# Changed loads, casts and sketch order in a polysketch attention and tanh-shrink FFN kernel

## The chip, the cores and the metric

The kernel runs on one core of a Trainium2 chip. The metric is the device time of one execution in microseconds (us); lower is better. Before the change it is 114.17 us, the median of three runs (113.98 to 114.34).

## What is computed

There are 4 batches, 4 heads, 1088 tokens and a head dimension of 32. The attention is linear: each q and k row is sketched by two 8 x 32 matrices, and the feature vector is the outer product of the two sketches (64 features).

```python
def phi(x):
    a = np.einsum('rd,bhsd->bhsr', S1, x)
    b = np.einsum('rd,bhsd->bhsr', S2, x)
    return np.einsum('bhsi,bhsj->bhsij', a, b).reshape(*x.shape[:-1], r * r)
q_p, k_p = phi(q), phi(k)
kv  = np.einsum('bhsf,bhsd->bhfd', k_p, v)
z   = np.sum(k_p, axis=2)
num = np.einsum('bhsf,bhfd->bhsd', q_p, kv)
den = np.einsum('bhsf,bhf->bhs', q_p, z)[..., None] + 1e-06
attn = num / den
```

The result, as x of shape 4352 x 128, goes through a layer without a gate, with w_in 128 x 2048 and w_out 2048 x 128:

```python
h = x @ w_in
out = (h - np.tanh(h)) @ w_out
```

## The kernel before, in words

**Order of the work.** The kernel does not issue instructions directly. Each step is added to a program (`P.add`) with the engines that may run it, an estimated duration, what it reads and writes, and a key (its priority). A list scheduler, `schedule`, then walks through an estimated time and gives every engine a fixed, in-order queue; `sync` adds the semaphores. An instruction that waits thus holds up everything behind it on its engine. Where TensorE would be idle in the plan, `fill` puts 128x256 matmuls on zeros (line 435) into its queue. The durations and the due times (`T_FIRST`, `PERIOD`, the keys) are constants at the top of the file.

**Loads.** All loads are added by `load` (line 466), in one order: k, q's first 8 of 34 chunks, v of batch 0; then the first quarter of W_in, the rest of q, three quarters of W_in, four quarters of W_out; then k, q and v of batches 1 to 3. They are issued by SyncE (the two small sketch matrices by ScalarE). `CAP` (1.4e6 bytes) bounds what is under way: a load waits for the landing of the one that would bring the sum over it. W_in comes in rows of 2 KB, W_out in pieces of 512 bytes. Both are f32 and are cast to bf16 in `weights` by ScalarE or GpSimd.

**Attention of a batch.** Here is the chain, with the names that the prediction uses.
- *kT, qT*: VectorE transposes k and q in blocks of 32 x 32 (lines 583, 592).
- *k sketch, kab*: TensorE multiplies by the sketch matrices (lines 599 and 610), VectorE transposes the result into `abk` (line 616).
- *gram, gm, scmm, sc*: small products that give what the denominator needs (lines 638, 642, 625, 648). From batch 1 on, scmm stands at the head of the kv product.
- *w*: three outer products on VectorE (line 659). *kv*: TensorE multiplies them by v (line 671). *kvd, kvt, kvb*: copy, transpose on TensorE, copy (lines 375, 703, 375).
- *q sketch, abc*: TensorE (line 724), then a VectorE transpose (line 729). *m, den, rd, ap*: the denominator and the divided sketch, on VectorE (lines 741 to 749).
- *qp, qpT*: outer products and their transposes on VectorE, 512 or 768 columns at a time (lines 767, 772). *num*: TensorE (line 783). *x*: two copies out of PSUM into the bf16 x, by VectorE or ScalarE (line 375).

Batch 0 is cut so that the first two of its nine blocks of 128 tokens give an early x: first k, w, kv and q's first piece, then the other seven blocks. The pieces in which num and x are done are in `PIECES`.

**FFN.** The 4352 rows of x are cut into ten groups of 256, 384, 448, six times 512, and 192. For each group, 16 *h* matmuls (line 877) each feed a tanh on ScalarE (line 881), and 16 + 2 *o* matmuls (lines 892, 896) sum up the output; the h @ w_out part is folded into one product W_c = w_in @ w_out, split into two bf16 halves, `wch` and `wcl` (lines 855 to 861; *wit* and *wiT* are the transposes of W_in that it needs). VectorE transposes the output (*ot*, line 901), and SyncE stores it. In the last three groups one tanh takes two banks (128 x 1024). The h matmuls use three PSUM banks, so TensorE can be three of them ahead of ScalarE.

Of the kernel before, what the change touches and what calls it, by code (L numbers as in the profile page):

```python
# [6 lines left out]
DM = 128  # L7
DFF = 2048
NJB = DFF // 128
NC = 34  # L10
# [12 lines left out]
CAP = 1.4e6  # L23
PAIRS = 7
URGENT = (-60500.0, 450.0)
PIECES = {0: [(0, 2), (2, 5), (5, 9)], 1: [(0, 5), (5, 9)], 2: [(0, 9)], 3: [(0, 9)]}
# [65 lines left out]
class _Prog:  # L92
# [58 lines left out]
    def schedule(self, filler=None):  # L151
# [31 lines left out]
        while n < len(self.ops):  # L183
# [33 lines left out]
            if e == "tensor":  # L217
                if o.name == "o0.0":
                    fills = False
# [7 lines left out]
            if o.dma:  # L227
                free[e] = t + occ
                wire = max(t + 1450.0, wire) + o.dma
                o.t1 = wire + (300.0 if o.key < -79000 else 2000.0)  # L230
            else:
                o.t1 = t + occ
                free[e] = o.t1
# [17 lines left out]
    def fill(self, filler, a, b):  # L251
        t = a
        while t + FILL[0] + FILL[1] < b:
            o = _Op()
            o.engs = {"tensor": (FILL[0], 215.0)}
# [3 lines left out]
            o.eng, o.t0, o.t1, o.lat = "tensor", t, t + FILL[0], 215.0  # L259
# [86 lines left out]
def bass_polysketch_attn__then__act_tanh_shrink_kernel(  # L346
# [43 lines left out]
    kL = [sb("kL", [128, NC * 32]) for _ in range(B)]  # L390
    vL = [sb("vL", [128, H, NB * 32]) for _ in range(B)]
    qL = [sb("qL", [128, NC * 32]) for _ in range(B)]
# [16 lines left out]
    NTH = 20  # L409
# [16 lines left out]
    wo_f = sb("wo_f", [128, NJB, DM])  # L426
    wi = [sbv("wi", [128, 512], BF16) for _ in range(4)]
    wo = [sbv("wo", [128, 4, DM], BF16) for _ in range(4)]
# [32 lines left out]
    for b in range(B):  # L461
        P.add(_v(128), lambda e, n, b=b: e.memset(vL[b][64:128, :, 256:288], 0.0), w=[vvals[b][1]], key=-89000 + b)
# [3 lines left out]
    def load(key, o_, i_, w, nbytes, eng="sync", rate=330.0, cap=True):  # L466
        after = []
        if cap:
            left = CAP - nbytes
            for op, nb in reversed(loads):  # L470
                left -= nb
                if left < 0:
                    after = [op]
                    break
        op = P.add({eng: (450.0, 0.0)}, lambda e, n: e.dma_start(out=o_, in_=i_), w=w, key=key, dma=nbytes / rate,
# [4 lines left out]
    for x, Sx in ((0, S1), (1, S2)):  # L480
        load(-99000 + x, sin.ap[:, x, :], Sx[None, :, :].to_broadcast([16, 8, 32]), [sin], 16384, "scalar")

    kvals = [[_Val(ap=kL[b].rearrange("p (r x) -> p r x", r=2)[:, :, e * 288:(544 if e else 288)]) for e in range(2)] for b in range(B)]
    qcut = {0: [0, 8, 34]}
# [3 lines left out]
    def load_k(key, b):  # L488
        src = k[b].rearrange("h (t r c) d -> (h t) r (c d)", r=2, c=17)
        if b == 0:  # L490
            for e in range(2):
                load(key + e, kvals[b][e].ap, src[:, :, e * 288:(544 if e else 288)], [kvals[b][e]], 128 * (256 if e else 288) * 8)
        else:
            load(key, kL[b][:, :], k[b].rearrange("h (t c) d -> (h t) (c d)", c=NC), kvals[b], 128 * 1088 * 4)

    def load_v(key, b):
        vs = v[b].rearrange("h (m x) d -> m h (x d)", x=17)
        for e in range(2):
            w_ = 256 if e else 288
            load(key + e, vL[b][e * 64:(e + 1) * 64, :, 0:w_], vs[:, :, e * 288:e * 288 + w_], [vvals[b][e]], 64 * w_ * 16)  # L500

    def load_q(key, b, i):
        a, z, val = qvals[b][i]
        src = q[b].rearrange("h (t c) d -> (h t) (c d)", c=NC)
        load(key, qL[b][:, a * 32:z * 32], src[:, a * 32:z * 32], [val], 128 * (z - a) * 128)

    wif = [_Val(ap=wi_f[:, i * 512:(i + 1) * 512]) for i in range(4)]
    wof = [_Val(ap=wo_f[:, i * 4:(i + 1) * 4, :]) for i in range(4)]
    wos = moe_w_out.rearrange("(jb ji) c -> ji jb c", jb=NJB, ji=128)

    def load_wi(key, i):
        load(key, wif[i].ap, moe_w_in[:, i * 512:(i + 1) * 512], [wif[i]], 128 * 2048)

    def load_wo(key, i):
        load(key, wof[i].ap, wos[:, i * 4:(i + 1) * 4, :], [wof[i]], 128 * 2048)
# [5 lines left out]
    load_wi(next(lk), 0)  # L521
    load_q(next(lk), 0, 1)
    for i in range(1, 4):
        load_wi(next(lk), i)
    for i in range(4):
        load_wo(next(lk), i)
    for b in range(1, B):
        load_k(next(lk), b)
        load_q(next(lk), b, 0)
        load_v(next(lk), b)  # L530

# [33 lines left out]
    xvals = []  # L565
    seq = [0]
# [6 lines left out]
    kT = [_Val(kT_p) for _ in range(B)]  # L573
    abk = [_Val(abk_p) for _ in range(B)]
# [5 lines left out]
    def k_transposes(b):  # L580
        for e_ in range(2):
            nb = NB - e_
            P.add(_v(nb * 64), lambda e, n, e_=e_, nb=nb: e.transpose(  # L583
                kT[b].ap.rearrange("p (j u t r) -> p r j u t", u=2, t=32, r=2)[:, :, 0:nb, e_, :],
                kL[b].rearrange("p (r j t) -> p r j t", r=2, t=32)[:, :, e_ * 9:e_ * 9 + nb, :]),
                r=[kvals[b][e_]], w=[kT[b]], key=nk(), name=f"kT{b}.{e_}")
# [7 lines left out]
    def k_sketch(b):  # L594
        _, pk = _group(att2, 2)
        for rh in range(2):
            def sk(e, n, rh=rh):
# [393 lines left out]
```

## Time and profile before

| what | us |
|---|---|
| median of three runs | 114.17 |
| the profiled execution | 114.65 |
| its span in the trace | 112.6 |
| TensorE matmul busy | 100.3 |
| ScalarE busy | 79.9 (tanh 69.5) |
| VectorE busy | 72.1 |
| GpSimd busy | 5.6 |
| first x complete | 18.96 |
| first tanh | 20.03 |
| last x copied from | 83.68 |

The span is the time between the first and the last instruction that the trace shows; some 2 us of the execution lie outside it. Times on a line of a timeline are counted from the start of the span. A line of a timeline gives the start, the duration, the engine, the source line, the operation, output and input and their number, and in brackets how long the engine was idle before and for whom. The chain of waits is followed back from the last instruction: at each step to what released it. Busy time of TensorE overlaps in the records, so that a TensorE shown as busy may still have room.

### The profile page before, as it was taken

How to read it: one execution, taken by the hardware profiler on the slowest of the kernel's cores; microseconds unless marked ns; L12 is line 12 of the kernel's file. 1: busy time of each engine (PE TensorE's matmuls, PEld its weight loads, DVE VectorE, ACT ScalarE, POOL GpSimd, SP SyncE). 2: the span in 40 equal slices, each digit the busy share in tenths (PEclk: the TensorE clock that was granted, in tenths of full speed). 3: DMA queues.
4: the chain of work that ended last, by engine and by line, in shares of the span. 5: the costliest groups of instructions: out<-in, count | busy, mean ns of one | idle time of the engine just before them, and what ended most of it. 6: DMA issues, size and time to landing. Idle time of an engine off the chain costs nothing.

```text
span 112.6 us, 3409 instructions
## 1 busy us (share of the span) xinstructions
PE 100.3 (89%) x1467; PEld 48.7 (43%) x1477; DVE 72.1 (64%) x115; ACT 79.9 (71%) x164; POOL 5.6 (5%) x25
## 2 busy tenths in 40 slices
PE   6975996998799989979999999979999999999960
PEld 4523783455355444436443346334243334334540
DVE  4469374899999999999999992499950020020030
ACT  2101247876487798586599867798969999999950
POOL 5202016000000000000000000000000000000000
PEclk9999999999999999999999999999999999999999
DMA  1999878799987804022000230005004106005035
GB/s 21 259 245 329 255 232 234 243 241 272 226 270 218 165 5 69 0 47 46 0 6 0 44 49 6 6 11 83 0 6 68 25 0 93 0 12 77 4 55 73
DMA packets 25037, 11.24 MB, mean 100 GB/s; under 512 B 18880, under 2 KB 23616, under 8 KB 25024
## 3 DMA queue, kind: packets, MB, share of 16 engines
q1 hardware_dynamic: 24320, 10.97, 40.7%
q8 instruction: 11, 0.18, 0.7%
q10 hardware_dynamic: 704, 0.08, 0.5%
q14 instruction: 2, 0.02, 0.1%
HBM read 8.81 MB, written 2.23 MB: 98 GB/s over the span
## 4 chain that ended last, share of the span: by engine, by line
PE 36%; ACT 28%; DVE 16%; DMA 13%; issue 2%; SPq 1%; DVEq 0%
ACT th L881 25%; PE psb L892 11%; PE psb L877 10%; DMA qL<-in_q_dram 5%; DMA wo_f<-in_moe_w_out_dram 5%; PE psb L783 5%; DVE qp L767 4%; DVE qpT L772 4%; DVE abc L729 3%; DMA kL<-in_k_dram 3%; PE psb L724 3%; PE psb L671 3%; DVE ot L901 2%; PE psb L610 2%; ACT wiT L375 2%
## 5 line engine op out<-in xcount | busy, mean ns | idle before, releaser
L881 ACT ACTIVATE th<-psb 128x512 bf16<-128x512 f32 (+4 forms) x136 | 69.5, 624 | 7.4 <-PE psb L877 6.6
L877 PE MATMUL psb<-xT,wi 128*128 128x512 bf16 (+4 forms) x155 | 50.1, 349 | 1.5 <-DVE xT L375 0.5
L892 PE MATMUL psb<-th,wo 128*128 128x512 bf16 (+4 forms) x157 | 48.2, 348 | 1.4 <-DVE ot L901 0.6
L877 PEld LDWEIGHTS psb<-xT,wi 128*128 128x128 bf16 x160 | 14.9, 97 | 25.3 <-ACT th L881 14.4
L892 PEld LDWEIGHTS psb<-th,wo 128*128 128x128 bf16 x160 | 14.6, 97 | 15.7 <-ACT th L881 7.5
L901 DVE STREAM_TRANSPOSE ot<-psb 128x512 f32<-128x512 f32 (+4 forms) x10 | 6.3, 626 | 22.6 <-PE psb L892 22.6
L772 DVE STREAM_TRANSPOSE qpT<-qp 128x768 f32<-128x768 f32 (+1 forms) x14 | 12.1, 861 | 0.4
L767 DVE TENSOR_TENSOR qp<-ap,abc 128x768 f32<-128x768 f32 (+1 forms) x14 | 11.5, 818 | 0.1
L659 DVE TENSOR_TENSOR w<-abk 128x768 f32<-128x768 f32 x12 | 11.3, 981 | 0.1
L729 DVE STREAM_TRANSPOSE abc<-psb 128x1152 f32<-128x1152 f32 (+2 forms) x5 | 5.7, 1143 | 5.1 <-PE psb L724 5.0
L435 PE MATMUL psb<-zz 128*128 128x256 bf16 x33 | 7.8, 388 | 1.1 <-DVE zz L434 1.1
L783 PE MATMUL psb<-qpT,kvb 32*32 32x128 f32 (+4 forms) x448 | 8.3, 309 | 0.1
L375 ACT CAST xT<-psb 128x192 bf16<-128x192 f32 (+4 forms) x8 | 3.3, 421 | 5.4 <-PE psb L783 5.4
L583 DVE STREAM_TRANSPOSE kT<-kL 128x576 f32<-128x576 f32 (+1 forms) x8 | 5.6, 724 | 1.7 <-DMA kL<-in_k_dram 1.7
L783 PEld LDWEIGHTS psb<-qpT,kvb 32*32 32x32 f32 x448 | 5.1, 103 | 2.9 <-DVE qpT L772 2.0
L671 PE MATMUL psb<-w,vL 128*32 128x64 f32 x288 | 6.0, 243 | 0.0
L592 DVE STREAM_TRANSPOSE qT<-qL 128x1088 f32<-128x1088 f32 (+2 forms) x5 | 5.3, 1055 | 0.9 <-DMA qL<-in_q_dram 0.9
L435 PEld LDWEIGHTS psb<-zz 128*128 128x128 bf16 x33 | 4.1, 135 | 3.6 <-DVE zz L434 1.1
L671 PEld LDWEIGHTS psb<-w,vL 128*32 128x32 f32 x288 | 5.1, 125 | 0.3 <-issue 0.2
L642 ACT COPY gm<-psb 128x32 f32<-128x32 f32 x4 | 0.8, 198 | 5.6 <-PE psb L638 5.6
L724 PE MATMUL psb<-qT,wq 32*32 32x288 f32 (+2 forms) x160 | 3.6, 381 | 0.9 <-ACT xT L375 0.9
L375 DVE CAST xT<-psb 128x192 bf16<-128x192 f32 (+3 forms) x6 | 2.8, 467 | 1.1 <-PE psb L783 1.0
(55 smaller groups left out, 56.6 us busy)
## 6 DMA issues: line engine op xcount, KB each, us to landing
kL<-in_k_dram SPq DMA_DIRECT2D x3, 544.0 KB, 3.6
qL<-in_q_dram SPq DMA_DIRECT2D x3, 544.0 KB, 4.9
vL<-in_v_dram SPq DMA_DIRECT2D x4, 288.0 KB, 4.8
vL<-in_v_dram SPq DMA_DIRECT2D x4, 256.0 KB, 5.0
wi_f<-in_moe_w_in_dram SPq DMA_DIRECT2D x4, 256.0 KB, 4.7
wo_f<-in_moe_w_out_dram SPq DMA_DIRECT2D x4, 256.0 KB, 5.8
out_dram<-ot SPq DMA_DIRECT2D x16, 64.0 KB, 2.0
out_dram<-ot SPq DMA_DIRECT2D x8, 56.0 KB, 1.9
```

The costliest lines, as they stand in the source:

```text
L375: return e.copy(o, i) if name == "scalar" else e.tensor_copy(o, i)
L435: filler = (lambda e, n: e.matmul(bank(3)[:, 0:256], zz.ap[:, 0:128], zz.ap[:, 128:384], start=True, stop=True), zop)
L659: P.add(_v(768), lambda e, n: e.tensor_tensor(out=wv.ap.rearrange("p (x i j) -> p x i j", i=8, j=8), in0=abh(0)[:, :, :, None].to_broadcas ...
L671: i = e.matmul(pv[b].ap[h * 32:(h + 1) * 32, 0:64], vL[b][:, h, blk * 32:(blk + 1) * 32], wvs[b, p].ap[:, (bi * 4 + h) * 64:(bi * 4 + h + ...
L729: P.add(_vp(sn * 4), lambda e, n: e.transpose(abc.ap.rearrange("p k h f -> p h k f")[:, :, 0:s1 - s0, :], psa4[:, :, 0:sn].rearrange("p h ...
L767: P.add(_v(cn * 256), lambda e, n, qp=qp, c0=c0, cn=cn: e.tensor_tensor(out=qp.ap[:, 0:cn * 256].rearrange("p (x i j) -> p x i j", i=8, j= ...
L772: P.add(_v(cn * 256), lambda e, n, qp=qp, o0=o0, cn=cn: e.transpose(qt.ap[:, o0 * 256:(o0 + cn) * 256], qp.ap[:, 0:cn * 256]), r=[qp], w=[ ...
L783: i = e.matmul(psa4[h * 32:(h + 1) * 32, g, 0:nb * 32], kvb.ap[g * 32:(g + 1) * 32, x, h * 32:(h + 1) * 32], qq[g * 32:(g + 1) * 32, 0:nb, ...
L877: P.add(_pe(n_ / 2.4 + 2.6), lambda e, n, jb=jb, hv=hv: e.matmul(hv.ap[:, jb % m * 512:jb % m * 512 + n_], wi[jb // 4].ap[:, (jb % 4) * 12 ...
L881: P.add(_a(n_ * m), lambda e, n, hv=hv, th=th: e.activation(out=th.ap.rearrange("p (u x) -> p u x", u=m)[:, :, 0:n_], in_=hv.ap.rearrange( ...
L892: fn = lambda e, n, x=x, st=st, sp_=sp_: e.matmul(ov.ap[:, 0:n_], wo[x // 4].ap[:, x % 4, :], ths[x][0].ap[:, ths[x][1] * 512:ths[x][1] * ...
L901: P.add(_vp(n_), lambda e, n: e.transpose(ot.ap[:, 0:n_], ov.ap[:, 0:n_]), r=[ov], w=[ot], key=-60000, name=f"ot{gi}")
```

## The change

The head loads are no longer capped, so nothing before batch 1 waits for a landing. `CAPS` holds two caps: one of 9.0e6 bytes for the head, and 1.4e6 for batches 1 to 3. W_in comes as two loads of 4 KB rows, and ScalarE alone casts it, in four steps that reorder its columns. W_out comes as two loads that GpSimd issues and that cast to bf16 on the way, in rows of 4 KB; the casts by ScalarE and GpSimd go. One of the two small sketch matrices is also loaded by GpSimd. There are k, q and v buffers for three batches in place of four: batch 3 takes those of batch 0, so its loads wait until batch 0 has been read.

In the order of the work: the first k sketch is split into two, one for each half of kT; scmm and its copy come before kv in all batches, in gram's bank; the k sketch of batch 1 and later must come after the q sketch of the batch before it (`qsk_last`), and the kT transposes after the last w (`wlast`); the x copies of batch 0's later pieces and of batch 1's first piece go to ScalarE alone; W_c is due earlier (`WKEY`); the first three h have a high priority; there are 36 buffers for tanh in place of 20. First x comes from two blocks, as before (`F0`). Fill matmuls are planned at half the duration from 6.3 us on and end at the first h. The scheduler's estimates for loads are changed too. Of what this makes of the queues: in GpSimd's, the three DMA issues stand ahead of the memset of `ident`; in VectorE's, the transpose and product that make the sketch weights stand ahead of the first kT, and the first half of kT of batch 1 stands ahead of abc of batch 0's last seven blocks; TensorE has 60 fill matmuls in place of 33; in ScalarE's, the wiT copies stand behind the first tanh.

```diff
-CAP = 1.4e6
+CAPS = (9.0e6, 1.4e6)
+WARM = 6300.0
+WKEY = (300.0, 300.0, 1500.0)
+F0 = 2
...
-    kL = [sb("kL", [128, NC * 32]) for _ in range(B)]
+    kL = [sb("kL", [128, NC * 32]) for _ in range(3)]
...
+    kL, vL, qL = kL + kL[0:1], vL + vL[0:1], qL + qL[0:1]
...
-    NTH = 20
+    NTH = 36
...
-        load(-99000 + x, sin.ap[:, x, :], Sx[None, :, :].to_broadcast([16, 8, 32]), [sin], 16384, "scalar")
+        load(-99000 + x, sin.ap[:, x, :], Sx[None, :, :].to_broadcast([16, 8, 32]), [sin], 16384, "gpsimd" if x else "scalar")
...
     def load_wi(key, i):
-        load(key, wif[i].ap, moe_w_in[:, i * 512:(i + 1) * 512], [wif[i]], 128 * 2048)
+        load(key, wif[i].ap, moe_w_in[:, i * 1024:(i + 1) * 1024], [wif[i]], 128 * 4096)
...
-        load(key, wof[i].ap, wos[:, i * 4:(i + 1) * 4, :], [wof[i]], 128 * 2048)
+        load(key, wo2[i].ap, moe_w_out[i * 1024:(i + 1) * 1024, :].rearrange("(p j) c -> p j c", j=8), [wo2[i]], 128 * 4096,
+             eng="gpsimd", issue=1000.0)
...
-            P.add(_v(nb * 64), lambda e, n, e_=e_, nb=nb: e.transpose(
+            P.add(_v(nb * 64), after=wlast, fn=lambda e, n, e_=e_, nb=nb: e.transpose(
...
-            P.add(_pe(485), sk2, r=[kT[b], wab], w=pk, key=nk(), mode="64x32", name=f"ksk{b}")
+            P.add(_pe(485), sk2, r=[kT[b], wab], w=pk, key=nk(), mode="64x32", name=f"ksk{b}", after=qsk_last)
...
+        P.add(_pe(80), lambda e, n: scmm(b, e), r=[s2r, gms[b]], w=[pg[b]], key=nk(), mode="128x32", name=f"scmm{b}")
...
-            P.add({**_a(kn * 64), **_vp(kn * 64)}, lambda e, n, hf=hf, kn=kn, xv=xv: copy(
+            P.add({**_a(kn * 64), **({} if 0 < b0 + b * 9 <= 9 else _vp(kn * 64))}, lambda e, n, hf=hf, kn=kn, xv=xv: copy(
...
-            P.add({**_as(512), **_g(512)}, lambda e, n, i=i: copy(e, n, wi[i].ap[:, :], wif[i].ap), r=[wif[i]], w=[wi[i]], key=-1000 + i, name=f"wi{i}")
-        for i in range(4):
-            last = P.add({**_as(512), **_g(512)}, lambda e, n, i=i: copy(e, n, wo[i].ap[:, :, :], wof[i].ap), r=[wof[i]],
-                         w=[wo[i]], key=T_FIRST + 100 + i, name=f"wo{i}")
+            P.add(_as(512), lambda e, n, i=i: copy(
+                e, n, wi[i].ap.rearrange("p (j f) -> p f j", j=4),
+                wif[i // 2].ap.rearrange("p (f j) -> p f j", j=8)[:, :, (i % 2) * 4:(i % 2 + 1) * 4]),
+                r=[wif[i // 2]], w=[wi[i]], key=-1000 + i, name=f"wi{i}")
...
-            P.add(_a(1024), lambda e, n, tp=tp, i=i: copy(
+            P.add({**_a(1024), **_v(1024)}, lambda e, n, tp=tp, i=i: copy(
...
-                after=[last], name=f"wc{jb}")
+                name=f"wc{jb}")
```

## The prediction

> **What bounds the kernel now.** I read the slices first: which engine is full in which part of the span.
>
> ```profile
> DVE  4469374899999999999999992499950020020030
> ACT  2101247876487798586599867798969999999950
> DMA  1999878799987804022000230005004106005035
> ```
>
> One digit is 2.8 us. VectorE is full from about 20 to 67 us, ScalarE only from about 84 us, the DMA engines in the first 35. So there are three stages: a head under the loads, a middle paced by VectorE's attention work, and a tail paced by ScalarE's tanh. The chain of waits says where one hands over to the next:
>
> ```profile
> 10.71 5.61 DMA wo_f<-in_moe_w_out_dram
> ...
> 16.34 0.62 ACT wo L375
> 16.96 1.83 ACT wiT L375 x2
> 18.79 0.18 ACT xT L375
> ...
> 19.10 0.81 PE psb L724 x32
> ...
> 19.94 1.13 DVE abc L729
> ...
> 82.11 1.53 PE psb L783 x63
> ...
> 84.43 20.98 ACT th L881 x28
> ```
>
> Columns: start, time on the chain, what. The head ends with a W_out load, its cast, the two wiT copies and only then ScalarE's half of the first x: everything in ScalarE's queue stands before that x. The q sketch of the rest of batch 0 waits for it, and VectorE for the sketch. The timelines of VectorE and ScalarE give the rest:
>
> ```profile
> 19.94 1.12 DVE L729 STREAM_TRANSPOSE abc<-psb 128x896 f32<-128x896 f32 x1 [1.78 <-PE psb L724]
> ...
> 70.64 0.42 DVE L375 COPY kvb<-psb 128x256 f32<-128x256 f32 x1 [2.48 <-PE psb L703]
> 72.38 1.38 DVE L729 STREAM_TRANSPOSE abc<-psb 128x1152 f32<-128x1152 f32 x1 [1.31 <-PE psb L724]
> ...
> 83.68 0.69 DVE L375 CAST xT<-psb 128x512 bf16<-128x512 f32 x1 [0.82 <-PE psb L783]
> ```
> ```profile
> 83.68 0.64 ACT L375 CAST xT<-psb 128x576 bf16<-128x576 f32 x1 [0.76 <-PE psb L783]
> 84.43 24.03 ACT L881 ACTIVATE th<-psb 128x512 bf16<-128x512 f32 x36
> ```
>
> The last x is copied at 83.68, then ScalarE works 24.03 us without a gap, and 4.1 us later the span of 112.6 ends. VectorE's waits in the middle (brackets) are mostly for TensorE. So the end is *last x + tanh still to do + 4.1*, and I work out each of the two anew.
>
> **Head.** *Loads.* Before and after, 3.77 MB come in ahead of batch 1. In the trace's packet records a 512-byte packet (W_out) takes 27 ns (median), a 2048-byte one (W_in) 84, a 4352-byte one (k, q) 168: 303, 390 and 414 GB/s on 16 engines. W_out's 2048 packets need 2048 x 27 / 16 = 3.5 us of the engines; as 256 rows of 4 KB at the rate of the 4352-byte packets, 256 x 158 / 16 = 2.5. Whether a casting load keeps that rate no row shows; I bound it by 2.5 and by twice that. More is won by the cap going: with k, q and v of batch 0 (640 packets of 1024 bytes at 65 ns, 512 of 1152 at 51, 128 of 3328 at 136: 5.3 us) and W_in (512 x 84 / 16 = 2.7) the head needs 11.5 us of packet time but runs to about 17, since SyncE waits for landings (W_in 2 to 4 issued at 7.94, W_out from 10.71). In the changed order only k of batch 1 waits. From 2.3 us on, with W_in's rows at the wide rate too, that is 10.4 us of packets, so W_in is complete by some 13 to 14.6 us, a landing's delay allowed. K of batch 1 now waits for W_out's first half alone; its transpose stands in VectorE's queue ahead of abc, at about 16, and if W_out were twice as slow (2.5 more) it would come some 2 us late and push abc by that.
>
> The Trainium skill speaks against the 4 KB rows (DMA: Bandwidth & Descriptors, Specifications): from 512 bytes on a transfer is at line rate. The rows above differ, 303 against 414 GB/s; by the page the 1.0 us of W_out would not be won, but the cap's part would.
>
> *GpSimd.* Three DMA issues now stand before the memset of ident on its queue. No row shows an issue there; on SyncE they take 0.33 to 1.27 us (W_out: four in 4.34). So ident's mask, ready for VectorE at 1.50 before, comes 1.0 to 3.8 us later. Behind it in VectorE's queue now stand stt and wab, and then the kT transposes (4.22 before): with 0.62 each (the sin issues on ScalarE) the mask is there at 3.4 and the transposes lose nothing; at 1.27 they lose 2 us. W_out also shares the engines with q and v of batch 0; q's first piece (6.90) may come 0.5 later. I take +0.3 for both, kab at 7.6.
>
> *From kab to the first x.* kab 0.85, then three w products: 3.11 us at 8.16 but 2.62 at 31.78, when GpSimd casts nothing; it casts nothing now, so w ends at 11.1 (11.27). TensorE stood 1.24 us before the kv product, its queue blocked by a transpose waiting for GpSimd's W_in cast; these 7+9 transposes now come after num. So the q sketch comes at 11.0, not 12.17, kv's last third ends by 12.1, kvd 0.37, kvt 0.69, kvb (on ScalarE) 0.37, with hand-overs 14.0. VectorE, from abc at 11.6, needs 3.93 us to the end of qpT (12.88 to 16.81) less 0.9 for kvb's wait and copy: 14.7. Num 0.85. ScalarE after kvb: four W_in casts at 0.62 = 2.5, so 16.5, then x 0.28: **first x whole at 16.8, before 18.96**. The casts now gather with a stride on both sides, which no row shows: I bound one by 0.62 and twice that and take the first, being the same engine and count. The wiT copies (1.92) move behind the first tanh. Two h matmuls and the sketch (0.81) later abc starts: **17.8, before 19.94**.
>
> The added fill matmuls (60 for 33) keep TensorE busy. The trace's fills are 0.215 us apart at 1 to 5 us and 0.117 at 16 us, and the first k sketch takes 1.22 us where later ones take 0.65 to 0.72. The Trainium skill's rule (TensorE: Matmul & The Clock Gate, Part 1) is full clock after about 3.4 us of sustained work; here 4.2 us of fills did not do it. By it the sketch would win 0.5 us. My sum takes none, because VectorE stands behind q's landing there. If the clock stays slow, 11 fills before num last 2.4 us instead of 1.3 and num is 1 us late, hidden behind the W_in casts.
>
> **Middle, by VectorE's changed order.** From abc of batch 0 to abc of batch 1: abc to ap 2.81, one 768 pair of qp and qpT 1.89, two 512 pairs 2.67, wcl 0.2, second half of kT 0.66, two qT 2.4, kab 0.85, ot 0.44, w 2.62: 14.5, hence abc at 32.3 (39.46 before, but there kT, qT, kab of batch 2 and a w came first, and here only qT). Batch 1 on: 3.2 + 1.9 + 3.9 + ot 0.5 = 9.5. Batch 2: kT 1.3, qT 1.2, kab 0.84, w 2.65, abc to ap 3.34, ot 0.6, three pairs 5.7 = 15.6. Batch 3: kT 1.3, x 0.65, kab 0.84, two ot 1.3, w 2.65, 3.34, 5.7 = 15.8. Sum 40.9. Off VectorE are four x copies and two or three kvb (2.4 us); they lie on ScalarE, which has idle time: 74.05 of 88.47 us are busy from 20.03 on.
>
> *Edits that I cost at nothing.* The batch 3 loads reuse batch 0's buffers and so wait for VectorE's and TensorE's reads of batch 0, done by 18; they were issued at 29 to 34 before, so the wait has 10 us of cover, and the output DMAs queued behind them on SyncE are first due at 30 and have three buffers. More tanh buffers (36 for 20) only let TensorE run ahead; uncovered, they are what lets 11 tanh be left for the tail, counted below. The sketch's small product moves ahead of kv, so that its copy no longer waits 0.4 to 0.7 for kv; the w products (2.6) hide either.
>
> Waits that I see: x of batch 2 for num (1.7 less 1.3 of kT3) 0.4; kab of batch 3 for its sketch, now behind the q sketch and both x copies, 0.7. Is TensorE in time? From the sketch of batch 1 to num of batch 3 it has 66 h and 74 o matmuls, 28.2 us at 0.165, 0.19 and 0.216 each, 11.4 us of attention and 14 mode changes of 0.16: 41.8, against 42.0 on VectorE. That is even, so I add 0.5 for hand-overs. Last num starts at 32.3 + 40.9 + 1.1 + 0.5 = 74.8; with 1.53 + 0.16 **the last x is copied at 76.5, before 83.68**.
>
> **Tail.** ScalarE's changed order has 23 single 512 tanh, 16 pairs and 8 short pairs behind that x; before it was 12, 16 and 8. A single is 0.498 (13 in 6.47), so 24.03 + 11 x 0.498 = 29.5 us. TensorE has 28.9 us there. End of tanh 76.5 + 0.65 + 29.5 = 106.7, before 108.46: **-1.8 us**. So 7.2 us at the last x shrink to 1.8, because 5.5 us of tanh that stood before it now stand behind it. Nothing changes in the last 4.1 us. Span 110.8; the profiled execution is 114.65, of which 2.05 lie outside the span, so 112.85. The median of the runs, 114.17, is 0.48 lower: **112.4**.
>
> **Rivals.**
> 1. *The waits go too.* No wait in the middle (-1.6) and abc at 17.3 (-0.5): 110.3. For it: the q-then-k order removes exactly the 2.48 and 1.31 waits of batch 3. Against: TensorE's 41.8 us leave no room.
> 2. *The loads are not sooner, or the strided casts are slow.* First x at about 18.9: with the casts from 14.0, that is 1.2 us a cast, or W_in complete at 17.4 at the old 250 GB/s. It costs the 2.1 us of the head: 114.5. Against: the packet times; 399 GB/s were reached at 9 to 10 us.
> 3. *Slower: the tanh left behind the last x.* With 29.5 us behind it the new order breaks even only if that x is copied by 78.3 (78.3 + 0.65 + 29.5 = 108.46). Before, VectorE waited 5.1 us in the middle (0.19 + 2.48 + 1.31 + 0.28 + 0.82); if that returns in place of my 1.6, x comes at 80.0 and the time is 115.9. For it: TensorE's queue is in order and full, and num stands behind 23 h matmuls. Against: w and the q transposes now fill VectorE while the sketches pass.
>
> **Numbers.** Forecast 112.4 with chance 0.44 (its own range 111.4 to 113.5), rival 1 0.26, rival 2 0.14, rival 3 0.16. A measurement of this kernel tells 0.3% (0.34 us) from no change. Faster: forecast, rival 1 and a little of rival 2: 0.72; the same: most of rival 2, 0.09; slower: rival 3 and the rest, 0.19. The range is 110.3 to 115.0: rival 1 at its edge and the milder half of rival 3 within.
>
> **What would show it.** Head: ScalarE's first x copy ends near 16.8 and abc of 28 columns starts near 17.8. Loads: no SyncE issue waits before k of batch 1; if VectorE's first kT is later than 4.6, GpSimd's issues are to blame. Middle: abc of batch 1 near 32.3, last x near 76.5, VectorE's waits under 2 us. Tail: 47 tanh in 29.5 us without a gap. Wrong would I be most through the middle, where three engines are even.

## The result, and the profile after

| | before | after |
|---|---|---|
| median of four runs each, one chip | 114.25 (113.98 to 114.50) | 123.62 (122.03 to 126.96) |
| profiled execution, and its span | 114.65, 112.6 | 122.03, 120.0 |
| k-a-b of batch 0 ready | 7.28 | 8.85 |
| kvb copied from | 15.04 | 14.37 |
| first x complete | 18.96 | 24.05 |
| abc of seven blocks | 19.94 | 25.95 |
| abc of batch 1 | 39.46 | 40.11 |
| last x copied from | 83.68 | 84.70 |
| tanh behind it | 24.03 | 29.47 |
| end of tanh to end of span | 4.1 | 5.3 |

After is slower by a ratio of 1.0725 (95% interval 1.0638 to 1.0813), against a forecast of 112.4. In this section and the next, ratios compare only runs in the faster of the two states that executions of one kernel fall into, while medians take all runs, so a ratio need not be the quotient of the medians beside it.

The slices of after (tenths busy, one digit is 3.0 us; PEclk is TensorE's granted clock):

```profile
DVE  2549853039999999989999599995202020020210
ACT  4001399947778679776799766898799999999920
PEclk9999996556999999999999999999999999999996
DMA  1999958859650201300130032005000505014034
```

VectorE's full middle and ScalarE's full tail are there as before, each some 8 us later than forecast. New is the hole: in the seventh digit and the eighth VectorE shows 3 and 0 while ScalarE shows 9, and the clock is near half from the seventh digit to the tenth. The chain of waits says what ScalarE does in the hole:

```profile
3.67 7.68 DMA vL<-in_v_dram
...
14.37 0.37 ACT kvb L381
14.74 9.21 ACT wi L381 x4
...
24.20 0.58 PE psb L888 x2
```

Four casts of W_in (`wi`, line 381) hold the chain for 9.21 us. The timelines of ScalarE and of VectorE:

```profile
14.64 9.31 ACT L381 CAST wi<-wi_f 128x512 bf16<-128x512 f32 x4
23.44 0.61 ACT L381 CAST xT<-psb 128x128 bf16<-128x128 f32 x1
...
84.69 0.64 ACT L381 CAST xT<-psb 128x576 bf16<-128x576 f32 x1 [0.82 <-PE psb L793]
85.23 29.47 ACT L892 ACTIVATE th<-psb 128x512 bf16<-128x512 f32 x47
```
```profile
8.48 0.45 DVE L604 STREAM_TRANSPOSE qT<-qL 128x256 f32<-128x256 f32 x1 [1.15 <-DMA qL<-in_q_dram]
...
25.95 1.12 DVE L739 STREAM_TRANSPOSE abc<-psb 128x896 f32<-128x896 f32 x1 [6.54 <-PE psb L733]
...
40.11 1.38 DVE L739 STREAM_TRANSPOSE abc<-psb 128x1152 f32<-128x1152 f32 x1
```

The casts start with the W_in that they need already landed (no bracket), stand 2.0 to 2.3 us apart, and ScalarE's half of the first x waits behind them, as the prediction had it, only with 9 us in place of 2.5. VectorE then waits 6.54 us for the sketch. TensorE's timeline:

```profile
17.61 0.74 PE L793 MATMUL psb<-qpT,kvb 32*32 32x64 f32 x51 [1.51 <-issue]
...
24.20 0.58 PE L888 MATMUL psb<-xT,wi 128*128 128x256 bf16 x2 [4.24 <-ACT xT L381]
```

TensorE has nothing for 4.24 us either, from 19.96 on. Its clock is half already before that. Here stretches of after (columns: stretch, length, then busy time and instructions of TensorE, its weight loads, VectorE, ScalarE, GpSimd, then clock, DMA share, GB/s):

```profile
15.40:18.81 3.41, 1.54 (x70) 0.98 (x68) 1.63 (x4) 3.41 (x2) 0.00 (x0) 1.00 0.34 127
...
19.00:24.00 5.00, 0.50 (x3) 0.24 (x3) 0.40 (x1) 5.00 (x4) 0.00 (x0) 0.50 0.99 278
24.00:30.00 6.00, 5.51 (x68) 3.21 (x69) 3.85 (x7) 3.79 (x10) 0.00 (x0) 0.58 0.79 234
```

The clock is half from 18.81 to 29.05 us. From abc on, the stretches are as long as forecast: 14.16 us to abc of batch 1 (14.5), 58.75 to the last x (58.7), 29.47 for the tail (29.5, the 47 tanh that were counted). At the very end SyncE's last six stores take longer. After, then before (start, length, queue, line):

```profile
113.87 4.08 SPq L922 DMA_DIRECT2D out_dram<-ot  x6
```
```profile
107.64 2.99 SPq L911 DMA_DIRECT2D out_dram<-ot  x6
```

One of after's six takes 1.60 us, where others take about 0.5.

### The profile page after: what moved, and what is told of

Read it like the earlier page. It is cut to its first block, busy times and chain, and to the rows that moved or that the text cites. A ratio compares the mean times of both kernels' runs of the same rounds, so it can differ in the third digit from the quotient of the medians.

```text
span 120.0 us, 3464 instructions
## 1 busy us (share of the span) xinstructions
PE 104.5 (87%) x1504; PEld 49.8 (42%) x1504; DVE 69.4 (58%) x108; ACT 88.9 (74%) x171; POOL 4.1 (3%) x23
## 4 chain that ended last, share of the span: by engine, by line
PE 40%; ACT 25%; DVE 20%; DMA 6%; SPq 2%; issue 2%; DVEq 0%
ACT th L892 14%; PE psb L888 13%; PE psb L903 12%; ACT wi L381 8%; DMA vL<-in_v_dram 6%; PE psb L793 6%; DVE w L670 4%; DVE qp L777 4%; DVE qpT L782 3%; DVE abc L739 2%; SPq L483 2%; PE psb L682 2%; DVE ot L912 2%; PE psb L625 2%; PE psb L733 2%
## 5 line engine op out<-in xcount | busy, mean ns | idle before, releaser
L888 PE MATMUL psb<-xT,wi 128*128 128x512 bf16 (+4 forms) x160 | 51.9, 354 | 5.1 <-ACT xT L381 4.2
L903 PE MATMUL psb<-th,wo 128*128 128x512 bf16 (+4 forms) x160 | 49.5, 352 | 0.5 <-DVE ot L912 0.5
L903 PEld LDWEIGHTS psb<-th,wo 128*128 128x128 bf16 x160 | 14.5, 98 | 16.1 <-ACT th L892 6.1
L443 PE MATMUL psb<-zz 128*128 128x256 bf16 x60 | 9.9, 320 | 1.1 <-DVE zz L442 1.1
L670 DVE TENSOR_TENSOR w<-abk 128x768 f32<-128x768 f32 x12 | 10.7, 950 | 0.1
L381 ACT CAST wi<-wi_f 128x512 bf16<-128x512 f32 x4 | 9.3, 2707 | 0.0
L443 PEld LDWEIGHTS psb<-zz 128*128 128x128 bf16 x60 | 6.3, 114 | 3.8 <-DVE zz L442 1.1
L381 ACT CAST xT<-psb 128x192 bf16<-128x192 f32 (+4 forms) x11 | 4.4, 435 | 3.7 <-PE psb L793 3.5
L682 PE MATMUL psb<-w,vL 128*32 128x64 f32 x288 | 5.1, 221 | 0.1
L682 PEld LDWEIGHTS psb<-w,vL 128*32 128x32 f32 x288 | 4.2, 110 | 1.7 <-DVE abc L739 1.1
L381 ACT COPY kvd<-psb 128x256 f32<-128x256 f32 x4 | 1.5, 372 | 3.9 <-PE psb L682 3.9
```

Source lines behind the costliest of these rows:

```text
L381: return e.copy(o, i) if name == "scalar" else e.tensor_copy(o, i)
L443: filler = (lambda e, n: e.matmul(bank(3)[:, 0:256], zz.ap[:, 0:128], zz.ap[:, 128:384], start=True, stop=True), zop)
L670: wlast[:] = [P.add(_v(768), lambda e, n: e.tensor_tensor(out=wv.ap.rearrange("p (x i j) -> p x i j", i=8, j=8), in0=abh(0)[:, :, :, None] ...
L682: i = e.matmul(pv[b].ap[h * 32:(h + 1) * 32, 0:64], vL[b][:, h, blk * 32:(blk + 1) * 32], wvs[b, p].ap[:, (bi * 4 + h) * 64:(bi * 4 + h + ...
L888: P.add(_pe(n_ / 2.4 + 2.6), lambda e, n, jb=jb, hv=hv: e.matmul(hv.ap[:, jb % m * 512:jb % m * 512 + n_], wi[jb // 4].ap[:, (jb % 4) * 12 ...
L903: fn = lambda e, n, x=x, st=st, sp_=sp_: e.matmul(ov.ap[:, 0:n_], wo[x // 4].ap[:, x % 8, :], ths[x][0].ap[:, ths[x][1] * 512:ths[x][1] * ...
```

## The experiments

Three theories stood to be told apart, and a fourth came up on the way. *1:* the casts write 256 bytes apart, and this costs four times a plain cast. *2:* W_out on GpSimd's queue is not free: it takes the DMA engines from k, q and v of batch 0. *3:* the long store at the end is a code fetch of SyncE, whose place depends on how many transfers it issues. *4:* the new order of the sketches only moves tanh behind the last x. Rivals to 1 were reads in pieces, a slow clock, and contention with the loads.

**m1_cast_patterns: what a pattern costs.** Only casts of 128x512 from f32 to bf16, on one engine after the other; everything else of the computation is left out. Two of the six patterns, writes 256 bytes apart and one f32 read in 32 bytes:

```diff
+        if n == "wrstep":
+            return d.rearrange("p (j f) -> p f j", j=4), s4
...
+        if n == "rdstep":
+            return d.rearrange("p (j f) -> p j f", j=4), src.rearrange("p (f j) -> p j f", j=8)[:, 0:4, :]
```

> The kernel leaves out the whole computation and only casts 128x512 f32 to bf16 on ScalarE, VectorE and GpSimd, twice each, in six access patterns: plain; reads in runs of 4 of every 8; writes 256 bytes apart; reads 32 bytes apart; reads 16 bytes apart; and the changed kernel's own (runs of 4 read, writes 256 bytes apart). Theory 1, the writes a stride apart are what makes the cast slow: the two patterns with such writes take about 2.3 us on ScalarE, the other four 0.62 to 0.8. Rival a, the short reads are slow: runs of 4 and reads 32 bytes apart take 2.3 us too. Rival b, neither is slow by itself and the 2.3 us in the changed kernel come from the loads that run beside it: all six near 0.62.

ScalarE's timeline (`plain`: nothing apart; `rdrun`: reads in runs of four f32; `wrstep` and `rdstep`: as above):

```profile
4.82 0.62 ACT L58 CAST plain_a<-src 128x512 bf16<-128x512 f32 x1 [2.81 <-DMA src<-in_moe_w_in_dram]
5.35 0.61 ACT L58 CAST rdrun_a<-src 128x512 bf16<-128x512 f32 x1
5.87 2.46 ACT L58 CAST wrstep_a<-src 128x512 bf16<-128x512 f32 x1
7.83 1.18 ACT L58 CAST rdstep_a<-src 128x512 bf16<-128x512 f32 x1
```

The change's own pattern (`both`) takes 2.46 as well. So it is the writes: runs of four f32 read at no cost, single f32 apart cost 1.9 times, bf16 written 256 bytes apart 4.0 times. GpSimd has the same 0.61, 2.46 and 1.13; VectorE 0.43, 1.30 and 0.70. Beside ScalarE's casts only stores of zeros run, beside GpSimd's no transfer and no other engine, and both take 2.46, so contention with loads is not the cause. A slow clock of TensorE is not either: in after the first of the four casts takes 2.48 while that clock is full. At m1's spacing (1.96 us from one such cast to the next instruction) four casts would hold the chain for 7.8 us; the other 1.4 of after's 9.21 are not explained by it. The Trainium skill (Advanced Engine Details and Errata, SBUF Cachelines) says that accesses which hit the same 16-byte line again run at full rate and others pay; the free runs of 16 bytes agree, and the size of the price comes from this run alone.

**e1_write_runs: the casts walk the other way.** Writes in a row, reads 32 bytes apart, else the change.

```diff
-                e, n, wi[i].ap.rearrange("p (j f) -> p f j", j=4),
-                wif[i // 2].ap.rearrange("p (f j) -> p f j", j=8)[:, :, (i % 2) * 4:(i % 2 + 1) * 4]),
+                e, n, wi[i].ap.rearrange("p (j f) -> p j f", j=4),
+                wif[i // 2].ap.rearrange("p (f j) -> p j f", j=8)[:, (i % 2) * 4:(i % 2 + 1) * 4, :]),
```

> The changed kernel with the same W_in casts walked in the other order, so that each writes 512 elements in a row and reads 32 bytes apart; the queues are the same. Theory 1, the strided casts cost 4 x 1.7 = 6.7 us on the path to the first x: a cast takes 0.62 to 0.8 us, the first x is whole at 17.2 to 18, abc of seven blocks starts at 18 to 19, TensorE's clock does not halve since it has no 4 us hole, the last x is copied at 77 to 78.5 and the time is 114.0 to 115.5, about 8 less than changed. Rival c, the loads at the head and the GpSimd issues cost it (kab at 8.85, not 7.28): the time stays above 120. Rival d, the order with 47 tanh behind the last x is what costs: the first x comes at 17 to 18 but the last one still after 81, time 117 to 120.

Measured: 119.21 (117.16 to 121.47), ratio 1.0326 [1.0225, 1.0426] to before. The four casts take 4.19 us, 1.01 to 1.03 from one to the next, close to m1's 1.09 for reads 32 bytes apart; first x whole at 20.06, abc at 21.83, last x 80.55. Half of the loss is gone; the expected 114.0 to 115.5 is missed, with k-a-b at 9.54, the clock half from 20.37 to 23.78, and the long store still at the end (5.2 us). ScalarE's timeline:

```profile
15.71 4.19 ACT L381 CAST wi<-wi_f 128x512 bf16<-128x512 f32 x4
19.80 0.26 ACT L381 CAST xT<-psb 128x128 bf16<-128x128 f32 x1
```

**e4_weights_strided: plain casts.** W_in is cast as it lies; TensorE picks its weights 16 bytes apart.

```diff
+    wcol = lambda jb: wi_b[jb // 8].rearrange("p (f j) -> p j f", j=8)[:, jb % 8, :]
...
-                e, n, wi[i].ap.rearrange("p (j f) -> p f j", j=4),
-                wif[i // 2].ap.rearrange("p (f j) -> p f j", j=8)[:, :, (i % 2) * 4:(i % 2 + 1) * 4]),
+                e, n, wi[i].ap[:, :], wif[i // 2].ap[:, (i % 2) * 512:(i % 2 + 1) * 512]),
...
-                    wi[jb // 4].ap[:, (jb % 4) * 128:(jb % 4 + 1) * 128], identb.ap[:, :]),
+                    wcol(jb), identb.ap[:, :]),
...
-                hv.ap[:, jb % m * 512:jb % m * 512 + n_], wi[jb // 4].ap[:, (jb % 4) * 128:(jb % 4 + 1) * 128], xt, start=True, stop=True),
+                hv.ap[:, jb % m * 512:jb % m * 512 + n_], wcol(jb), xt, start=True, stop=True),
```

> The changed kernel with plain W_in casts; TensorE reads the W_in columns 16 bytes apart instead when it loads weights for h and for the W_in transposes. Theory 1: casts 0.62, head as in the run with writes in a row; if strided weight loads cost nothing that they don't hide behind a matmul, the time is 114.0 to 115.5. If a weight load takes four times its 97 ns, it is longer than a 512 matmul's 216 and 160 of them add up to 0.2 us each, some 30 us: 145.

Measured: 118.15 (116.28 to 119.44), ratio 1.0262 [1.0156, 1.0369]. The casts take 0.62 and stand 0.52 apart, 2.18 us for four: the 2.5 that the forecast took. A weight load from `wi` takes 145 ns for 97, and the h matmuls keep their spacing (median 0.216 us). Yet the time comes down by 5.5 only, and the profile shows why: in this execution (119.00 us; the shortest took 116.28) the first x is whole at 21.51, because k-a-b is ready at 11.57. VectorE's timeline:

```profile
4.95 0.77 DVE L597 STREAM_TRANSPOSE kT<-kL 128x576 f32<-128x576 f32 x1
9.55 0.71 DVE L597 STREAM_TRANSPOSE kT<-kL 128x512 f32<-128x512 f32 x1 [3.83 <-DMA kL<-in_k_dram]
```

The second half of k, issued like before's, lands after 8.1 us; before it took 3.6, and 5.1 in after. That is theory 2's place. e9 below has the same head and a shorter execution (117.41), and k-a-b is late there too, at 10.30:

```profile
7.04 0.71 DVE L597 STREAM_TRANSPOSE kT<-kL 128x512 f32<-128x512 f32 x1 [1.39 <-DMA kL<-in_k_dram]
9.93 0.45 DVE L606 STREAM_TRANSPOSE qT<-qL 128x256 f32<-128x256 f32 x1 [2.18 <-DMA qL<-in_q_dram]
10.30 0.80 DVE L633 STREAM_TRANSPOSE abk<-psb 128x288 f32<-128x288 f32 x2
```

**e5_before_uncapped: the cap alone.** Before, with only the head loads uncapped.

```diff
-            left = CAP - nbytes
+            left = CAPS[1 if key >= -89880 else 0] - nbytes
```

> The kernel before with the cap off its head loads alone (up to 9.0e6 bytes; batches 1 to 3 keep 1.4e6); the queues are the same. Theory 1 puts nothing of the loss on the cap: W_in complete at about 14 in place of 14.5, W_out 1 to 2 us sooner, first x at 17.5 to 18.9, time 112.5 to 114.2. Rival c, more loads in flight hold up k, q and v of batch 0 (kab 8.85 in the changed kernel, 7.28 before): kab at 8 or later, and the time 114.5 to 117.

Measured: 114.28 (113.99 to 114.54), ratio 1.0027 [0.9992, 1.0062]. k-a-b at 6.69, first x whole at 18.96 as in before, last x 83.37. ScalarE's wiT copies do come a microsecond sooner (15.86 for 16.87), but its x then waits 0.88 us for num. The cap's going neither hurts nor helps by itself.

**e6_wout_held: theory 2.** e4, and W_out's two loads on GpSimd wait for v of batch 0 to land.

```diff
-             eng="gpsimd", issue=1000.0)
+             eng="gpsimd", issue=1000.0, more=(v0,))
```

> Plain W_in casts with strided weight loads as in e4, and W_out's two loads by GpSimd wait until v of batch 0 has landed. Theory 2: what is left of the loss after the casts is that W_out, on its own queue from 3 us on, shares the engines with k, q and v of batch 0 (kab at 8.85 in the changed kernel, 9.54 and 11.57 in e1 and e4, 7.28 before and 6.69 in e5, whose cap is off too but whose W_out stands behind them in the same queue). Then kab comes at 7.0 to 7.6, abc of seven blocks at 17 to 18.5, last x 76 to 77.5, time 112.5 to 114.5. Rival e, GpSimd's three issues ahead of ident are what delays kab: they are gone here as well, since the two issues now stand behind ident; the two are told apart by what VectorE waits for in the trace of e4 (a landing of k or q, not ident). Rival f, TensorE's code loading is what sets it: num still breaks off for 1.3 to 1.5 us and the first x stays behind 19.

Measured: 115.04 (113.88 to 117.08), ratio 1.0076 [1.0036, 1.0117]: from e4, 3.1 us by the medians and 1.9% by the ratios. VectorE's timeline, against that of e4 above:

```profile
5.01 1.36 DVE L598 STREAM_TRANSPOSE kT<-kL 128x576 f32<-128x576 f32 x2
...
7.19 0.48 DVE L634 STREAM_TRANSPOSE abk<-psb 128x288 f32<-128x288 f32 x1 [0.49 <-PE psb L616]
```

No landing is waited for any more; first x whole at 15.5, abc at 16.8, a microsecond ahead of the forecast's head. So theory 2 holds for this kernel, though the last x, at 78.55, and the time come later than expected (76 to 77.5, 112.5 to 114.5). (The hold also puts the issues behind `ident`, whose mask comes at 2.71 in place of 3.83; but kT starts at 4.95 in e4 and 5.01 here, so that is not the gain.) It agrees with the Trainium skill (DMA: Bandwidth & Descriptors, Issuing engines are not separate DMA queues): transfers of all issuing engines run on the same 16 DMA engines. The end has no long store here and stands at 4.4 for e4's 5.0, so some 0.6 us of the gain are the end's and not the head's. Beside e9, whose head is e4's, the last tanh ends 2.4 us sooner (107.62 for 110.02).

**e7_win_four_loads.** e6 with W_in in four loads of 2 KB rows, so that a quarter can be cast when it is there; and two transfers of SyncE more, for theory 3.

```diff
-        load(key, wif[i].ap, moe_w_in[:, i * 1024:(i + 1) * 1024], [wif[i]], 128 * 4096)
+        load(key, wif[i].ap, moe_w_in[:, i * 512:(i + 1) * 512], [wif[i]], 128 * 2048)
```

> e6 with W_in in four loads of 2 KB rows, as before, in place of two, so that two more DMAs stand on SyncE ahead of the output. Theory 3: the 1.2 us by which the changed kernel's end trails the last tanh more than before (5.3 against 4.1) are one fetch of SyncE's code that falls among the last six stores (one issue of 1.6 us, with an instruction fetch at 114.3); two more DMAs ahead move it into the wait before those stores, and the stretch from the last tanh to the end is 4.1 again: 1 us less than e6, 111.5 to 113.5. Rival: the stretch is 5.0 to 5.3 whatever the number of DMAs, and the time that of e6 within 0.5.

Measured: 114.10 (113.52 to 115.07), ratio 1.0024 [0.9988, 1.0060]. First x whole at 15.79, abc 17.09, last x 78.34, end 4.4. The first cast starts at 11.05 in place of 11.56, but the last ends within 0.2 us of e6's, the rest of the profile is e6's within 0.3 us, and the two profiled executions took 114.08 and 114.10: the better median is not explained by what the four loads do at the head. Since e6 had lost the long store already, the run says nothing on theory 3, and the 1 us that was expected of it did not come.

**e8_no_sketch_order.** e6 without the two order rules (the k sketch after the q sketch, kT after w).

```diff
-            P.add(_v(nb * 64), after=wlast, fn=lambda e, n, e_=e_, nb=nb: e.transpose(
+            P.add(_v(nb * 64), fn=lambda e, n, e_=e_, nb=nb: e.transpose(
...
-            P.add(_pe(485), sk2, r=[kT[b], wab], w=pk, key=nk(), mode="64x32", name=f"ksk{b}", after=qsk_last)
+            P.add(_pe(485), sk2, r=[kT[b], wab], w=pk, key=nk(), mode="64x32", name=f"ksk{b}")
```

> e6 without the two order rules (k sketch behind the q sketch before it, kT behind the last w). Theory 4: the new order gains 5 us from the first abc of seven blocks to the last x and gives them back in tanh left behind that x (88.5 us from that abc to the last tanh before, 88.7 to 89.1 in the changed kernel, e1 and e4), so without it the stretch from abc to the last tanh is 88 to 89.5 and the time that of e6 within 1. Rival d, the order costs: 2 us or more less than e6. Rival g, the order helps: 2 us or more slower.

Measured: 114.15 (113.64 to 115.53), ratio 1.0048 [1.0002, 1.0094]. Last x at 76.22, 2.3 us before e6's, but now 49 tanh stand behind it in place of 45, and tanh ends at 107.25, e6's at 107.62. The order rules decide where the tanh are done, and hardly the end.

**e9_two_more_loads: theory 3.** e4, with k of batches 1 and 2 in two loads each, so that SyncE issues 68 transfers in place of 66.

```diff
-        if b == 0:
+        if b < 3:
```

> The kernel is the one with plain casts and strided weight loads (118.15, last stretch 5.0 us from the end of the last tanh to the span's end), with k of batches 1 and 2 loaded in two parts each, so that SyncE issues two loads more, as many as before. Theory that the number of SyncE's transfers decides where its code fetch falls: no store of the last six takes over 700 ns, the last stretch is 4.1 to 4.5 us, and the time is 0.5 to 1 us below 118.15. Rival, that the fetch comes at that place whatever the number: a store of 1.2 to 1.6 us again, a last stretch of 5.0, and the time within 0.5 of 118.15.

Measured: 118.29 (117.41 to 119.12), ratio 1.0394 [1.0343, 1.0444]; the last six stores take 4.03 us, one of them 1.57, and the last stretch is 5.3. Theory 3 as I put it falls. What the traces do show: in after, e1, e4 and e9 the instruction queue brings 12 blocks and the long store is the same one, the 67th of SyncE's 73 recorded instructions (in after a block starts at 114.32, beside the store of 1.60 that starts at 114.23); in before and in the other variants of it and of the change it brings 11, and the end has none. Why e6 needs one block less is open.

**e10_four_loads_cap and e13_four_loads_no_order: the cap in the middle.** Both are e7 without the order rules. In e10 batches 1 to 3 have 2.6 MB under way in place of 1.4; TensorE, VectorE, ScalarE and GpSimd have the same instructions in the same order.

```diff
-CAPS = (9.0e6, 1.4e6)
+CAPS = (9.0e6, 2.6e6)
```

> The kernel with plain casts, W_out held until v of batch 0 has landed and W_in in four loads (114.10), without the two order rules of the q and k sketches, and with the loads of batches 1 to 3 let on at 2.6 MB in flight in place of 1.4. Theory that VectorE's waits for late loads of batches 1 and 2 hold the middle: these waits fall below 0.5 us, last x is copied at 75.5 to 77, and the time is 112.5 to 113.6. Rival, that TensorE has no free time in the middle, whatever VectorE waits for: last x at 76 to 78, the end of tanh within 0.4 of 107.3, and the time 113.8 to 114.5.

> The kernel with plain casts, W_out held until v of batch 0 has landed, W_in in four loads, and no order rules for the q and k sketches, with the loads of batches 1 to 3 at 1.4 MB in flight as before. It differs from the one at 2.6 MB (118.48) in nothing but when SyncE starts loads; the order of instructions on TensorE, VectorE, ScalarE and GpSimd is the same. Theory that TensorE's stall of 3.5 us at 25.9 to 29.4 there, put down to no semaphore, with the DMA engines at 99 to 100%, was a code load behind full queues: with the smaller cap the stall is under 1 us, the clock is full from 30 on, and the time is 113.0 to 114.1, so the cap cost 4 us or more. Rival, that the stall belongs to this order of instructions: 2 us or more of it again, and 117 or more. And whether the two repairs add up: four loads gave 0.94 us and no order rules 0.89 from 115.04, so 113.2 if they do, about 114.1 if both only uncover the same TensorE-bound middle.

Measured: e10 118.48 (116.33 to 119.38; the profiled execution took 118.78), ratio 1.0298 [1.0227, 1.0369]; e13 113.55 (112.69 to 115.25), ratio 0.9979 [0.9925, 1.0032]. In e10 VectorE waits for no landing from 20 us on, as expected, but the time is beyond both expectations and the ratio 3.2 points worse than e13's. TensorE's timeline in e10, then in e13:

```profile
29.37 0.64 PE L796 MATMUL psb<-qpT,kvb 32*32 32x128 f32 x5 [3.50 <-issue]
```
```profile
26.54 0.41 PE L796 MATMUL psb<-qpT,kvb 32*32 32x128 f32 x5 [1.10 <-issue]
```

It is the same place in the program in both, between the 59th and the 60th of 64 num matmuls. "issue" means that no semaphore explains the wait. The stretch 26 to 30 us of e10, then of e13:

```profile
26.00:30.00 4.00, 0.63 (x6) 0.25 (x6) 1.90 (x3) 0.00 (x0) 0.00 (x0) 0.81 1.03 305
```
```profile
26.00:30.00 4.00, 3.31 (x34) 1.66 (x34) 2.68 (x6) 2.72 (x8) 0.00 (x0) 1.00 0.82 206
```

With the DMA engines full, the stall is three times as long; the clock is half from 28.47, within the stall, to 35.3 in e10, never there in e13, and abc of batch 1 comes at 37.85 for 32.72. It fits code that is fetched through the same engines (in e10 the instruction queue moves a block at 26.6), but no row names whose code that was, and each stall is read from one execution. The two repairs of e7 and e8 come to 1.49 us together (115.04 to 113.55, where 113.2 was expected of a full sum); neither alone is clear of e6's interval, so whether they add up is not shown. That e13 is 0.2% below before is inside its interval, so no version that beats before is shown. ScalarE's tail in e13:

```profile
75.98 0.64 ACT L381 CAST xT<-psb 128x576 bf16<-128x576 f32 x1 [1.60 <-PE psb L796]
76.52 30.49 ACT L894 ACTIVATE th<-psb 128x512 bf16<-128x512 f32 x49
```

**e11_before_wout_gpsimd: W_out's part alone, on before.** Uncapped as e5; W_out by four casting loads of GpSimd, not held, its casts gone (to match W_out's rows, TensorE picks its W_in weights 8 bytes apart, which the lines below leave out).

```diff
-        load(key, wof[i].ap, wos[:, i * 4:(i + 1) * 4, :], [wof[i]], 128 * 2048)
+        load(key, wo[i].ap, moe_w_out[i * 512:(i + 1) * 512, :].rearrange("(p j) c -> p j c", j=4), [wo[i]], 128 * 2048, eng="gpsimd")
...
-        for i in range(4):
-            last = P.add({**_as(512), **_g(512)}, lambda e, n, i=i: copy(e, n, wo[i].ap[:, :, :], wof[i].ap), r=[wof[i]],
-                         w=[wo[i]], key=T_FIRST + 100 + i, name=f"wo{i}")
```

> The kernel before, with its head loads uncapped (114.28), and of the rest of the change only W_out's: four casting loads of 2 KB rows issued by GpSimd at the start, W_out's casts gone. W_in stays as it was. Theory that W_out on a queue of its own takes the DMA engines from k and q of batch 0: k-a-b is ready at 8.3 us or later in place of 6.7, with VectorE waiting for k or q rather than for the identity, and the time is 114.6 to 117. Rival, that the damage of the whole change was the W_in casts alone: k-a-b at about 7, and the time at or below 114, since the casts of W_out are gone.

Measured: 114.43 (113.78 to 117.46), ratio 1.0032 [0.9999, 1.0065]. Theory 2's place is there, k-a-b at 9.48 for 6.69, with 1.61 us waited for k and 0.61 for q; its price is not. First x is complete at 18.9 all the same and the last x at 83.19. In this schedule the 2.8 us are hidden: in e5 VectorE waits 2.89 us for the q sketch before the first abc (13.16), in e11 it does not, and abc comes at 12.97. In e4's schedule, as e9 shows it, that wait is 0.38 us, so there a late k-a-b delays the first x.

**e12_before_strided_casts: the casts' pattern alone, on before.** ScalarE and GpSimd share them, as before; the rows of W_out are loaded to match.

```diff
-            P.add({**_as(512), **_g(512)}, lambda e, n, i=i: copy(e, n, wi[i].ap[:, :], wif[i].ap), r=[wif[i]], w=[wi[i]], key=-1000 + i, name=f"wi{i}")
+            P.add({**_as(512), **_g(512)}, lambda e, n, i=i: copy(
+                e, n, wi[i].ap.rearrange("p (j f) -> p f j", j=4), wif[i].ap.rearrange("p (f j) -> p f j", j=4)),
+                r=[wif[i]], w=[wi[i]], key=-1000 + i, name=f"wi{i}")
```

> The kernel before, with only the pattern of the W_in casts changed: they write 256 B apart as in the change (and the rows of W_out are loaded in the order that goes with it), while they stay shared between ScalarE and GpSimd and all queues stay as they were. Theory that the strided writes alone carry most of the loss: 2.0 to 2.5 us a cast in place of about 0.6, the transposes of W_in late, the first x copied 3 to 6 us after 18.96, and 116 to 121 us in all. Rival, that with two engines at it the casts lie beside other work: first x within 1.5 us of before's, and 114.5 us or less.

Measured: 116.53 (115.85 to 116.80), ratio 1.0231 [1.0195, 1.0267]. GpSimd's timeline has

```profile
9.57 2.46 POOL L375 CAST wi<-wi_f 128x512 bf16<-128x512 f32 x1 [4.14 <-DMA wi_f<-in_moe_w_in_dram]
14.05 2.46 POOL L375 CAST wi<-wi_f 128x512 bf16<-128x512 f32 x1 [2.02 <-DMA wi_f<-in_moe_w_in_dram]
```

and ScalarE's two take 2.48. The time is in theory 1's band, the first x is only 2.3 us late (21.3): with two casts to an engine, partly beside the wait for W_in, the pattern costs 2.6 us of the end, where four in a row took 6.7 from the head of after. Part of the delay comes by VectorE, and GpSimd casts nothing in after: beside the first of these casts the last of VectorE's three w products takes 2.61 us, for 1.36 in before and 0.95 beside no cast, and the three take 4.35 for 3.11:

```profile
7.86 4.35 DVE L659 TENSOR_TENSOR w<-abk 128x768 f32<-128x768 f32 x3
```

## Why the prediction was wrong, by its own steps

- **"ScalarE after kvb: four W_in casts at 0.62 = 2.5": the step that failed.** It measured 9.2 on the chain. The prediction saw that no row showed the pattern, and still bounded it "by 0.62 and twice that", "being the same engine and count". Neither bound had a reason: 0.62 was a row of another pattern, and the double was a guess. m1 gives 2.46 for the pattern (7.8 us of the 9.2; why three of after's four took 2.78 is open), e4 gives back 5.5 us of the median with plain casts and the strided weight loads that go with them, and e12 loses 2.3% with the pattern and W_out's matching rows, though partly by VectorE. In after's profile the forecast's 17.8 for abc became 25.95: 0.37 at kvb, 6.7 in the casts, 0.33 in the x copy (0.61 for 0.28), and 0.9 from x to abc, at half clock (the parts overlap by 0.2).
- **Rival 2** ("the strided casts are slow", 1.2 us a cast, 114.5) was the right mechanism at half its size, and so it ended as no change. By its own rule (the head's delay is the end's delay) 2.3 a cast would have given 112.4 + 6.7 = 119.1.
- **"I take +0.3 for both, kab at 7.6"**: 8.85 in after, 11.57 in e4, 10.30 in e9, 7.19 with W_out held. GpSimd's issues themselves were inside the bounds (mask at 3.83; the first kT at 4.95, 0.73 late). "q's first piece may come 0.5 later" was the small part of it: VectorE waited 0.91 for k and 1.15 for q. In after's profile the casts stand behind and only 0.37 of it is left at kvb; once the casts are plain, holding W_out is worth 2 to 3 us (e4 to e6, by ratios or medians), some 0.6 of it at the end.
- **Loads**: "W_in complete at 13 to 14.6" was near: its halves landed 8.4 and 9.2 us after their issue, at 13.4 and 14.7, and no cast waited for them. W_out's 256 packets took 3.0 us of the 16 engines, between the two bounds. "If the clock stays slow ... hidden behind the W_in casts": TensorE's clock was full from 5.15 to 18.81, but its stall of 1.51 in num (not foreseen) was hidden behind the casts as such.
- **"My sum takes none" for the clock**: for the fills this was right, and around the hole that the casts make it left out ten microseconds of half clock. The Trainium skill (TensorE: Matmul & The Clock Gate, Part 1) has the gate close after an idle window of about 3.4 us. Here it closes sooner: after's clock is half from 18.81, before the hole of 4.24 us begins, and TensorE was busy 1.54 of the 3.41 us ahead of that; e10's is half from 28.47, 2.6 us into its stall of 3.50.
- **Middle and tail**: 14.16, 58.75 and 29.47 against 14.5, 58.7 and 29.5. The count of VectorE's changed order and of the 47 tanh was right. That 58.75 meets 58.7 is in part luck: with an early head the same stretch takes 61.75 in e6, 61.25 in e7, 59.19 in e8 and 59.11 in e13. Rival 3's returning waits did not come in after; its break-even (last x by 78.3) was missed by 6.4 us for another reason.
- **"Nothing changes in the last 4.1 us"**: 5.3, by one store of SyncE. No row of before could show it.
- **Would 112.4 have been right with the casts plain?** No. With both faults of the head gone, e6, e7, e8 and e13 are at 113.6 to 115.0. e13 comes nearest to the forecast's plan: abc 16.87 (17.8), last x 75.98 (76.5), but 49 tanh instead of 47, end of tanh 107.0 (106.7), span 111.4 (110.8). An earlier head does not reach the end: in e6 from abc to abc of batch 1 it is 16.8 us for 14.16 in after, since VectorE then waits 1.79 us for q of batch 2, and in e13 TensorE is busy 9.98 of the 10 us from 30 to 40. Loading more at once costs more than it brings (e10).

## What to carry to other kernels

When an edit gives an instruction an access pattern that no row shows, the duration of the same engine and count is no bound: look at which side is written or read apart, and take the reordering out of the cast altogether if a later instruction, here TensorE's weight load, can do it beside other work. A transfer moved to another engine's queue still takes its share from those that the critical path waits for, so hold it until these have landed. And before an early stage is made faster, ask which stage behind it has no free time left: here 3.1 us at the head (abc at 16.80 in e6 for 19.94 in before) were worth 0.8 at the last tanh (107.62 for 108.46).

## What the runs showed of the hardware

- A cast of 128x512 from f32 to bf16 that writes 256 bytes apart takes 2.46 us on ScalarE and GpSimd and 1.30 on VectorE, for 0.61 and 0.43. Reading one f32 in 16 or 32 bytes takes 1.17 and 0.70, reading runs of four nothing more. In after three of the four casts took 2.78, and the x copy behind them 0.61 for 0.26; why is open.
- Beside a GpSimd cast that writes 256 bytes apart, VectorE's product of two tiles, 128x768, takes 2.61 us in e12, for 1.36 beside the plain cast in before and 0.95 alone.
- TensorE's weights may lie 16 bytes apart: 145 ns a load for 97, hidden beside the h matmuls (0.216 us apart in e4 as in after).
- TensorE can stand at one place of its program with no semaphore to wait for: 1.10 us in e13 and 3.50 in e10 at the same matmul, with the DMA engines full in e10; 0.47 in e5 and 1.51 in after inside num, where before's profile has none. Full DMA engines are not needed: in after their share is 0.45 from 16 to 17 us and 0.05 from 17 to 17.6, while TensorE stands.
- TensorE's granted clock can fall to half with no long hole before it: in after at 18.81, behind 3.41 us of which TensorE was busy 1.54, in e1 at 20.37, behind 3.41 us of which it was busy 1.61.
